# A fused attention, mixer and expert kernel: value products of the last stage begun a step later, output projections queued behind the next projections

## The chip, the cores and the metric

One core of one Trainium2 chip runs the whole program in one launch. The metric is device microseconds of that core; the kernel before took 782.88 us (median of three runs, 781.44 to 784.33). The engines are TensorE (PE, with its weight loads as PEld), VectorE (DVE), ScalarE (ACT), GpSimd (POOL) and SyncE (SP), which issues the DMAs.

## The reference

Three layers on four batches of 576 positions, in float32:

```python
# 1. attention on q, k, v (4, 8, 576, 64): banded part plus a part pooled by 4; 2. mixer over tokens and channels
# 3. four experts, each a causal attention of its own (x is 4 x 576 x 512, wq/wk/wv 512 x 64, wo 64 x 512)
logits = x @ w_gate                                   # the top 2 of 4 get softmax weights w
for e in range(E):
    q = x @ wq[e]; k = x @ wk[e]; v = x @ wv[e]
    scores = np.where(causal, -1e9, scale * (q @ k.transpose(0, 2, 1)))
    a = softmax(scores)                               # max taken off, 1e-9 added to the sum
    ye = a @ v @ wo[e]
    out += mask[..., None] * w[:, :, kk:kk + 1] * ye  # where expert e is one of the top 2
```

## The kernel before, in words

The first two layers fill the first 560 us or so; the change leaves their instructions in the same order on every engine. The last stage is the third layer. It goes through eight pairs, here called pair 0 to pair 7: batch 0 experts 0 and 1, batch 0 experts 2 and 3, batch 1 experts 0 and 1, and so on. Even pairs open a batch, odd pairs close one.

For each pair there are ten score tiles (five tiles of 116, the last of 112, query positions, times two experts), in the order 4, 3, 2, 0, 1 (`TORD`). A loop over 14 steps issues, at step n, the score tile n (`score`: three or more matmuls into PSUM, then on DVE the maximum `nm`, on ACT the exponential into a tile `Pc`, on DVE the normalisation with the gate) and, four steps later (`LAG`), its transposes (`turn`: PE into `pt`, ACT copies into `PT`). When all tiles of one half of the positions are turned, `attend` multiplies `PT` by the values `VV` into `o`: 10 matmul pairs of experts for the later half (at step 9), 6 for the earlier half (at step 13, the pair's last). In the trace these are the `o<-PT,VV` runs of 20 and 12 records.

Beside that, every step takes one item or more from a list `fill`. Its items are the four projections of the next pair (`proj`: K and Q, two halves each, 12 matmuls), for odd pairs also the value projections (`v_proj`) and gates of the next batch, and for even pairs from 2 on the five output projections (`project_out`: 6 matmuls into `wo`, an ACT copy into a tile `y`, a DMA of `y` to the output) of the batch just finished. In pairs 2 and 4 the output projections stand at the head of the list, in pair 6 (`HOLD`) behind the four projections. `split_x` takes each batch's activations apart into `vh` (ACT, `vh<-u`) and `vlo` (POOL); it has six buffers for four tiles per batch, so it is placed where the projections of the batch before have let go of them.

`y` and `Pc` share one tag of eight buffers (`PCB`), PSUM has six single banks and one double one, and SP issues all DMAs in order. A scheduler sets each engine's order from program order, priorities (`ahead`) and its own estimate of durations; each engine then works strictly in that order and waits on semaphores. `chain` keeps the matmuls of one run in their order on PE without a wait.

Of the kernel before, what the change touches and what calls it, by code (L numbers as in the profile page):

```python
# [65 lines left out]
def body(ctx, tc, qT, kT, vw, vp, wt1, wt2, wc1, wc2, wq, wk, wvg, wo, out):  # L66
# [25 lines left out]

        return nc.vector if i < VEC.get(kind, 0) else nc.gpsimd

    def chain(run):

        for x, y in zip(run, run[1:]):
            tc.add_manual_dep(y.ins, x.ins.name, mybir.DependencyInfo(mybir.DependencyClass.NoSync,
                                                                      mybir.DependencyReason.DATA), reason="chain")

    cst = pool("cst")
    ident = cst.tile([128, 128], F32, name="ident")
# [39 lines left out]
    def mm3(ps, terms, first=True, last=True):  # L142
        n = 3 * len(terms)
        i = 0
        for (lh, ll), (rh, rl) in terms:
            for a, c in ((lh, rh), (lh, rl), (ll, rh)):
                nc.tensor.matmul(ps, a, c, start=first and i == 0, stop=last and i == n - 1)  # L147
                i += 1

    def flat(t, shape):  # L150
# [133 lines left out]
    def scores(b, p):  # L284
# [20 lines left out]

        ps = b2("sl")
        for h in range(2):
            nc.tensor.matmul(ps[:, h, :NW * 32].rearrange("p (t k) -> p t k", k=WIN), identb,
                             band[:, None, :].to_broadcast([128, NW // 2, WIN]), start=True, stop=False)
        for w in range(NW):  # L310
            o, g = 64 * (w % 2), 2 * (w // 2)
            cols = slice(KS[w], KS[w] + WIN)

            for h0, h1 in [(0, 2)] if g != NT - 1 else [(0, 1), (1, 2)]:
                bk, c0 = (g + h0) // NT, (g + h0) % NT * WIN
                nc.tensor.matmul(ps[o:o + 64, bk, c0:c0 + (h1 - h0) * WIN].rearrange("p (h k) -> p h k", k=WIN),  # L316
                                 qt[:, cols], kz[:, h0:h1, cols], start=False, stop=(g + h1) % NT == 0)
        sv = ps[:, :, :NW * 32].rearrange("p b (t k) -> p b t k", k=WIN)
        nmx = pa.tile([128, 2, NT], F32, tag="nmx", bufs=3, name="nmx")
# [14 lines left out]
        sd = b2("sd")  # L334
        for h in range(2):
            for c in range(2):
                nc.tensor.matmul(sd[:72, h, c * SD:(c + 1) * SD], qd[64 * h:64 * h + 64, c * 72:(c + 1) * 72],
                                 kd[64 * h:64 * h + 64, :], start=True, stop=True)
        sdv = sd[:72, :, :2 * SD].rearrange("p h (c k) -> p h c k", c=2)
        nd = pa.tile([72, 2, 2], F32, tag="nd", bufs=3, name="nd")  # L340
# [16 lines left out]
    def turns(b, p):  # L357
        P, Pd = SC.pop((b, p))
        PdT = pa.tile([112, 3, SD], F32, tag="PdT", bufs=2, name="PdT")
        pd = b1("pdt")  # L360
        for i, (k0, k) in enumerate(PK):
            k = min(112, 2 * SD - k0)
            for c in range(2):
                o = i * SD + c * 72
                nc.tensor.transpose(pd[:k, o:o + 72], Pd[:, c].rearrange("p h k -> p (h k)")[:, k0:k0 + k], ident[:72, :72])
        nc.scalar.activation(PdT[:, :2].rearrange("p c k -> p (c k)"), pd[:112, :2 * SD], AF.Copy)
        nc.scalar.activation(PdT[:96, 2], pd[:96, 2 * SD:3 * SD], AF.Copy)
        PT = pa.tile([128, NT, 128], F32, tag="PT", bufs=2, name=f"PT{b}_{p}")
        for t0, t1 in ((0, 3), (3, 5)):
            ps = b1("tl")  # L370
            for t in range(t0, t1):
                nc.tensor.transpose(ps[:, (t - t0) * 128:(t - t0 + 1) * 128], P[:, t], ident)
            nc.scalar.activation(PT[:, t0:t1].rearrange("p t q -> p (t q)"), ps[:, :(t1 - t0) * 128], AF.Copy)
        TR[b, p] = (PT, PdT)

    def values(b, p):
        PT, PdT = TR.pop((b, p))
        po = b1("pod")
        vd, vx = Vd[b, p]
        for h in range(2):  # L380
            k = PK[2 * h][1]
            nc.tensor.matmul(po[64 * h:64 * h + 64, :SD], vd[:k, h], PdT[:k, 2 * h], start=True, stop=False)
        nc.tensor.matmul(po[:, :SD], vx.rearrange("p h d -> p (h d)"), PdT[:, 1], start=False, stop=True)
        OdT = pa.tile([128, SD], F32, tag="OdT", bufs=2, name="OdT")
        nc.scalar.activation(OdT, po[:, :SD], AF.Copy)
        up = OdT[:, :, None].to_broadcast([128, SD, 4])
        for w0, w1 in ((0, 4), (4, NW)):
            o = b1("ol")
            s0 = w0 * WQ
            s1 = min(w1 * WQ, S)  # L390
            for w in range(w0, w1):
                q0 = w * WQ
                n = min(WQ, S - q0)
                r0 = 64 * (w % 2) + q0 - KS[w]
                for h in range(2):
                    nc.tensor.matmul(o[64 * h:64 * h + 64, q0 - s0:q0 - s0 + n], Vl[b, p][:, h, w],  # L396
                                     PT[:, w // 2, r0:r0 + n], start=True, stop=True)
            nc.vector.tensor_tensor(U[b][:, p, s0:s1].rearrange("p (g r) -> p g r", r=4),
                                    o[:, :s1 - s0].rearrange("p (g r) -> p g r", r=4),
                                    up[:, s0 // 4:s1 // 4], op=OP.add)  # L400
# [3 lines left out]
    def tok_turn(b, hf):  # L404
        xs = []
        for g in range(3):
            ts = [2 * g, 2 * g + 1] if g < 2 else [4]
            tn = TS[ts[0]]
            ps = b1(f"tx{g}")
            psv = ps.rearrange("p (t d) -> p t d", t=2)  # L410
            for i, t in enumerate(ts):
                for j in range(2):
                    nc.tensor.transpose(psv[:tn, i, j * 128:(j + 1) * 128],
                                        U[b][:, 2 * hf + j, TQ * t:TQ * t + tn], ident)
            hi = pt.tile([TQ, len(ts), 256], F32R, tag=f"xh{g}", bufs=1, name="xh")
            lo = pt.tile([TQ, len(ts), 256], F32R, tag=f"xl{g}", bufs=1, name="xl")
            n = len(ts)
            split(hi[:tn, :n], lo[:tn, :n], psv[:tn, :n])
            xs += [(hi[:tn, i], lo[:tn, i]) for i in range(n)]
        TK[b, hf] = xs  # L420
# [270 lines left out]
    def score(b, p, t, e):  # L691
# [11 lines left out]
            sv = ps[:nq, :, :HS]  # L703
        for ps, a0, a1 in parts:
            m0, m1 = max(d0, a0), min(d0 + nq, a1)
            nc.tensor.matmul(ps[:nq, :a1 - a0], Q[:, qs], K1[:, a0:a1], start=True, stop=False)  # L706
            nc.tensor.matmul(ps[:nq, :a1 - a0], Q[:, qs], K2[:, a0:a1], start=False, stop=m0 >= m1)
            if m0 < m1:
                nc.tensor.matmul(ps[:nq, m0 - a0:m1 - a0], identb[:nq, :nq], caus[:nq, m0 - d0:m1 - d0],  # L709
                                 start=False, stop=True)  # L710
        nm = pc.tile([TQ, 1], F32, tag="nm", bufs=6, name="nm")
        su = pc.tile([TQ, 1], F32, tag="su", bufs=6, name="su")
# [15 lines left out]
    def turn(b, p, t, e):  # L728
# [4 lines left out]
        for c0, c1 in [(0, t + 1)] if t < 4 else [(0, 4), (4, 5)]:  # L733
            pt = b1("pt")
            for c in range(c0, c1):
                nc.tensor.transpose(pt[:TS[c], (c - c0) * TQ:(c - c0) * TQ + nq], P[:nq, c * TQ:c * TQ + TS[c]],  # L736
                                    ident[:nq, :nq])
            v = pt[:, :(c1 - c0) * TQ].rearrange("p (c q) -> p c q", q=TQ)[:, :, :nq]
            m = min(c1, 3)
# [7 lines left out]
    def attend(b, p, s):  # L747
# [4 lines left out]
        q0, q1 = s * HS, (s + 1) * HS  # L752
        o = b1("o")
        cs = [c for c in range(NT) if c * TQ < q1]
        run = []

        for c in cs:
            a = max(q0, c * TQ)
            for e in (1, 0):
                ec = (2 * p + e) * 64  # L760
                run.append(nc.tensor.matmul(o[64 * e:64 * e + 64, a - q0:q1 - q0], ST[b]["VV"][:TS[c], c, ec:ec + 64],  # L761
                                 PT[e][:TS[c], column(c, a):column(c, a) + q1 - a], start=(c == 0), stop=(c == cs[-1])))
        chain(run)
        oh, ol = ST[b]["OT"][p]
        split(oh[:, q0:q1], ol[:, q0:q1], o[:, :HS])

# [17 lines left out]
    if PRE:  # L784
        for k, s in parts:
            proj(0, 1, k, s)
    fill, held, later = [], [], []
    tiles = [(t, e) for t in TORD for e in range(2)]
    for i, (b, p) in enumerate(pairs):
        nxt = pairs[i + 1] if i + 1 < len(pairs) else None  # L790
        if nxt:
# [5 lines left out]
            if nxt[1] == 0:  # L797
                fill += [lambda t=t, n=nxt: v_proj(n[0], t) for t in range(NT)]
                fill += [lambda n=nxt: gates(n[0])]
        if i >= HOLD or nxt is None:  # L800
            fill, held = fill + held, []
        steps = len(tiles) + LAG
        last = nxt is None
        if last:
# [3 lines left out]
                [lambda t=t, b=b: project_out(b, t) for t in range(NT)])  # L808
        wait = [{(t, e) for t, e in tiles if t * TQ < (s + 1) * HS and t * TQ + TS[t] > s * HS} for s in range(2)]
        for n in range(steps):  # L810
            if n < len(tiles):
                with ahead("s"):
                    score(b, p, *tiles[n])
            if n >= LAG:
                with ahead("t"):
                    turn(b, p, *tiles[n - LAG])
                for s in range(2):
                    if tiles[n - LAG] in wait[s]:
                        wait[s].remove(tiles[n - LAG])
                        if not wait[s]:  # L820
                            with ahead("a"):
                                attend(b, p, s)
                            if last:
                                for t in range(NT):
                                    if s in todo[t]:
                                        todo[t].remove(s)
                                        if not todo[t]:
                                            fill.append(lambda t=t: project_out(b, t))
            left = max(1, steps - FRONT - n)
            for _ in range(-(-len(fill) // left)):  # L830
                with ahead("f"):
                    fill.pop(0)()
        fill += later
        later.clear()
    for f in fill:
        f()

# [52 lines left out]
```

## Time and profile before

| | |
|---|---|
| runs before | 782.88 us median (781.44 to 784.33) |
| the profiled execution | 780.84 us, span 779.0 us |
| mean granted TensorE clock | 0.963 of full speed |
| PE busy, whole span | 697.4 us (90%) |
| last stage, from the first value product to the end | 576.9 to 779.0 us |

The profile comes from one execution. A line of the timeline gives start, duration, engine, source line, operation, output and inputs, the number of records merged, and in brackets how long the engine had been idle before it and what it waited for. Busy PE time is modelled at the ends of matmuls, so idle times are the surer reading. A granted clock of 1.00 is 2.4 GHz, 0.50 is 1.2 GHz; a window's figure is a mean over it.

### The profile page before, as it was taken

The page shows a single profiled execution, that of the slowest core. Times are in us where ns is not written, and L with a number is a line of the kernel's source. Part 1 is how long each engine was busy: PE and PEld are TensorE (multiplying, and loading weights), DVE is VectorE, ACT ScalarE, POOL GpSimd, SP SyncE. Part 2 cuts the span into 40 slices and gives each one's busy share as a digit, 9 for nine tenths or more (in the row PEclk, how much of TensorE's full clock was granted, in tenths as well). Part 3 has the DMA queues.
Part 4 walks back from the last instruction along what each step waited for, and adds up shares of the span by engine and source line. Part 5 has one row for each costly group of instructions (what it writes and reads, how often), then busy time and mean ns, then how long its engine had stood idle before and what let it go on. Part 6 is the DMA issues. An engine that isn't in the chain of part 4 may idle for free.

```text
span 779.0 us, 15384 instructions
## 1 busy us (share of the span) xinstructions
PE 697.4 (90%) x5784; PEld 632.3 (81%) x5784; DVE 482.4 (62%) x1203; ACT 398.5 (51%) x1321; POOL 164.8 (21%) x196
## 2 busy tenths in 40 slices
PE   4266889999999999999999999999989989989983
PEld 2245667788899999999999999999979769778762
DVE  3686989555455966854664455443487567577560
ACT  5466686566543625522542233332376466566661
POOL 4477787443101302100200000004030020010000
PEclk9578989999999999999999999999999999999998
DMA  7777755431001301300110010000201111220201
GB/s 215 195 207 206 225 182 167 111 111 47 19 1 33 131 1 59 105 1 1 56 55 1 1 42 14 1 2 1 50 13 32 50 48 28 64 57 4 66 28 61
DMA packets 31586, 52.39 MB, mean 67 GB/s; under 512 B 3544, under 2 KB 16344, under 8 KB 31512
## 3 DMA queue, kind: packets, MB, share of 16 engines
q1 hardware_dynamic: 31512, 51.40, 23.1%
q8 instruction: 46, 0.75, 0.4%
q14 instruction: 28, 0.23, 0.1%
HBM read 41.95 MB, written 4.72 MB: 60 GB/s over the span
## 4 chain that ended last, share of the span: by engine, by line
PE 67%; DVE 11%; DMA 10%; ACT 7%; SPq 2%; issue 2%; ACTq 0%; DVEq 0%
PE c L147 34%; PE proj L147 5%; DMA wc_raw<-in_wc_dram 4%; PE vp L147 4%; PE o L761 4%; PE h L147 4%; DMA out_dram<-y 3%; PE pu L147 3%; PE ol L396 2%; ACT Pc L716 2%; PE sl L316 2%; PE wo L147 2%; PE pt L736 2%; DMA vz<-in_vw_dram 2%; PE s L706 1%
## 5 line engine op out<-in xcount | busy, mean ns | idle before, releaser
L147 PE MATMUL c<-ul,wch 128*128 128x288 f32 x384 | 113.7, 296 | 0.9 <-DVE ul L522 0.9
L147 PE MATMUL c<-uh,wch 128*128 128x288 f32 x384 | 113.5, 296 | 0.4 <-DVE acc L545 0.4
L147 PE MATMUL c<-hh,wch 128*128 128x288 f32 x384 | 113.9, 297 | 0.0
L147 PE MATMUL c<-hl,wch 128*128 128x288 f32 x384 | 113.4, 295 | 0.0
L147 PE MATMUL c<-hh,wcl 128*128 128x288 f32 x384 | 113.2, 295 | 0.0
L147 PE MATMUL c<-uh,wcl 128*128 128x288 f32 x384 | 113.1, 295 | 0.0
L130 ACT ACTIVATE hh<-c 128x288 fp32r<-128x288 f32 x96 | 39.1, 408 | 120.7 <-PE c L147 120.7
L136 DVE SCALAR_TENSOR_TENSOR hl<-c,hh 128x288 fp32r<-128x288 f32 x96 | 43.3, 452 | 63.7 <-ACT hh L130 63.7
L147 PEld LDWEIGHTS c<-ul,wch 128*128 128x128 f32 x384 | 72.4, 188 | 1.8 <-DVE ul L522 1.8
L147 PEld LDWEIGHTS c<-uh,wch 128*128 128x128 f32 x384 | 72.1, 188 | 0.9 <-DVE acc L545 0.9
L147 PEld LDWEIGHTS c<-hl,wch 128*128 128x128 f32 x384 | 72.3, 188 | 0.1
L147 PEld LDWEIGHTS c<-hh,wch 128*128 128x128 f32 x384 | 72.2, 188 | 0.2
L147 PEld LDWEIGHTS c<-hh,wcl 128*128 128x128 f32 x384 | 72.3, 188 | 0.0
L147 PEld LDWEIGHTS c<-uh,wcl 128*128 128x128 f32 x384 | 72.3, 188 | 0.0
L193 POOL TENSOR_TENSOR wc_t<-wc_f,wc_t 128x512 int32<-128x512 int32 x24 | 33.7, 1408 | 168.9 <-ACT wc_t L183 156.6
L521 ACT ACTIVATE uh<-u 128x288 fp32r<-128x288 f32 x128 | 52.9, 441 | 27.4 <-PE c L147 27.4
L522 DVE TENSOR_TENSOR ul<-u,uh 128x288 fp32r<-128x288 f32 x128 | 56.5, 469 | 8.8 <-ACT uh L521 8.7
L327 ACT ACTIVATE P<-sl,nmx 128x64 f32<-128x64 f32 x160 | 48.3, 333 | 19.7 <-DVE nmx L321 19.6
L716 ACT ACTIVATE Pc<-s,nm 112x576 f32<-112x576 f32 (+4 forms) x80 | 44.5, 559 | 25.9 <-DVE nm L713 14.4
L713 DVE TENSOR_REDUCE nm<-s 112x1 f32<-112x576 f32 (+4 forms) x80 | 40.4, 515 | 10.9 <-PE s L709 10.1
L625 POOL TENSOR_TENSOR vlo<-u,vh 128x576 fp32r<-128x576 f32 x16 | 22.6, 1448 | 90.8 <-ACT vh L624 90.8
L761 PE MATMUL o<-PT,VV 116*64 116x288 f32 (+4 forms) x256 | 29.4, 375 | 12.2 <-ACT PT L741 12.2
(171 smaller groups left out, 1828.6 us busy)
## 6 DMA issues: line engine op xcount, KB each, us to landing
wc_raw<-in_wc_dram SPq DMA_DIRECT2D x24, 512.0 KB
vp<-in_vp_dram SPq DMA_DIRECT2D x16, 336.0 KB
vz<-in_vw_dram SPq DMA_DIRECT2D x32, 160.0 KB
qT<-in_qT_dram SPq DMA_DIRECT2D x16, 288.0 KB
kz<-in_kT_dram SPq DMA_DIRECT2D x32, 144.0 KB
kT<-in_kT_dram SPq DMA_DIRECT2D x16, 288.0 KB
K<-K SPq DMA_DIRECT2D x64, 72.0 KB
out_dram<-y SPq DMA_DIRECT2D x16, 232.0 KB
```

The lines of the kernel that those rows point to most:

```text
L130: nc.scalar.activation(hi, src, AF.Relu if relu else AF.Copy, **({"scale": scale} if scale else {}))
L136: nc.vector.scalar_tensor_tensor(lo, src, 0.0, h, op0=OP.max, op1=OP.subtract)
L147: nc.tensor.matmul(ps, a, c, start=first and i == 0, stop=last and i == n - 1)
L193: nc.gpsimd.tensor_tensor(flat(dst, shape).bitcast(I32), f, t.bitcast(I32), op=OP.add)
L316: nc.tensor.matmul(ps[o:o + 64, bk, c0:c0 + (h1 - h0) * WIN].rearrange("p (h k) -> p h k", k=WIN), qt[:, cols], kz[:, h0:h1, cols], start= ...
L327: nc.scalar.activation(P[:, t, h], sv[:, bk, i], AF.Exp, bias=nmx[:, bk, i:i + 1], scale=0.125, accum_out=sm[:, t, h:h + 1])
L521: nc.scalar.activation(hi, u, AF.Copy)
L522: getattr(nc, ULO).tensor_tensor(lo, u, hi.bitcast(F32), op=OP.subtract)
L625: getattr(nc, XLO).tensor_tensor(lo, U[b][:, c], hi.bitcast(F32), op=OP.subtract)
L713: nc.vector.tensor_reduce(nm[:nq], sv, axis=AX.X if t < 4 else AX.XY, op=OP.max, negate=True)
L716: nc.scalar.activation(pv_, sv, AF.Exp, bias=nm[:nq], accum_out=su[:nq])
L761: run.append(nc.tensor.matmul(o[64 * e:64 * e + 64, a - q0:q1 - q0], ST[b]["VV"][:TS[c], c, ec:ec + 64], PT[e][:TS[c], column(c, a):column ...
```

## The change

All matmuls and transposes now go through `mm` and `tp`, which note the last one issued. While `order["on"]` is set (in `attend`), each matmul is kept behind the one issued just before it in the program, the first of the run included. This replaces `chain`, which kept only the run together.

`attend` is no longer called where its last tile is turned, except in the last pair. It goes into `due` and is called at the end of the next step, after that step's score, turn and `fill` items. For the later half that is step 10, in which no score is left. For the earlier half it is step 0 of the next pair.

The output projections of a finished batch are no longer put into `fill` at the end of the odd pair. They wait in `later` and `ready` and join `fill` at step 1 of the even pair, behind its projections.

```diff
+    def behind(ins):
+
+        if order["on"]:
+            tc.add_manual_dep(ins.ins, order["last"].ins.name,
+                              mybir.DependencyInfo(mybir.DependencyClass.NoSync, mybir.DependencyReason.DATA),
+                              reason="order")
+        order["last"] = ins
+
+    def mm(*a, **kw):
+        behind(nc.tensor.matmul(*a, **kw))
...
-        if i >= HOLD or nxt is None:
-            fill, held = fill + held, []
...
         for n in range(steps):
+            now, due = due, []
...
-                        if not wait[s]:
+                        if not wait[s] and not last:
+                            due.append((b, p, s))
+                        elif not wait[s]:
                             with ahead("a"):
                                 attend(b, p, s)
...
+            if n == 1:
+                fill, ready = fill + ready, []
+                if i >= HOLD or last:
+                    fill, held = fill + held, []
             left = max(1, steps - FRONT - n)
             for _ in range(-(-len(fill) // left)):
                 with ahead("f"):
                     fill.pop(0)()
-        fill += later
-        later.clear()
+            for a in now:
+                with ahead("a"):
+                    attend(*a)
+        ready, later = ready + later, []
```

On TensorE at the end of pair 1, the run of the earlier half stood right behind the last two transposes and ahead of the output projections of batch 0 (line 736 is `turn`, 761 `attend`, 147 `mm3`):

```order
L736 MATMUL pt<-ident,Pc 116x116 x2
L761 MATMUL o<-PT_7150,VV 64x288
L761 MATMUL o<-PT_7149,VV 64x288
L761 MATMUL o<-PT_7150,VV 64x172
L761 MATMUL o<-PT_7149,VV 64x172
L761 MATMUL o<-PT_7150,VV 64x56
L761 MATMUL o<-PT_7149,VV 64x56
L147 MATMUL wo<-wo_hi,oh 116x512
L147 MATMUL wo<-wo_lo,oh 116x512
L147 MATMUL wo<-wo_hi,ol 116x512
```

In the changed program twelve matmuls of a K projection stand between those transposes and the run (the last four of them are shown; line 106 is now `mm`, for all):

```order
L106 MATMUL proj<-vh,wk_hi 128x288
L106 MATMUL proj<-vh,wk_hi 128x288
L106 MATMUL proj<-vlo,wk_hi 128x288
L106 MATMUL proj<-vh,wk_lo 128x288
L106 MATMUL o<-PT_7150,VV 64x288
L106 MATMUL o<-PT_7149,VV 64x288
L106 MATMUL o<-PT_7150,VV 64x172
L106 MATMUL o<-PT_7149,VV 64x172
L106 MATMUL o<-PT_7150,VV 64x56
L106 MATMUL o<-PT_7149,VV 64x56
L106 MATMUL proj<-vh,wk_hi 128x288
L106 MATMUL proj<-vlo,wk_hi 128x288
```

The run has moved behind one projection; the output projections have left this place altogether.

On ScalarE at the start of pair 2 there stood the copies of the output projections, one between each two exponentials (line 773 is the copy into `y`, 716 the exponential, 741 and 745 the copies of transposes):

```order
L130 ACTIVATE oh<-o 128x288
L773 ACTIVATE y<-wo 116x512
L716 ACTIVATE Pc,su<-s,nm 112x576
L773 ACTIVATE y<-wo 116x512
L716 ACTIVATE Pc,su<-s,nm 116x464
L773 ACTIVATE y<-wo 116x512
L716 ACTIVATE Pc,su<-s,nm 116x464
L773 ACTIVATE y<-wo 116x512
L741 ACTIVATE PT_7458<-pt 116x3x112
L745 ACTIVATE PT_7458<-pt 116x112
L745 ACTIVATE PT_7458<-pt 112x112
L716 ACTIVATE Pc,su<-s,nm 116x348
```

Now the copies of K and Q stand there (line 140), and four copies `vh` of the next batches (line 634):

```order
L140 ACTIVATE oh<-o 128x288
L140 ACTIVATE K_7831<-proj 64x288
L726 ACTIVATE Pc,su<-s,nm 116x464
L140 ACTIVATE K_7832<-proj 64x288
L140 ACTIVATE Q_7829<-proj 64x288
L634 ACTIVATE vh<-u_91 128x576 x2
L634 ACTIVATE vh<-u_92 128x576
L726 ACTIVATE Pc,su<-s,nm 116x464
L140 ACTIVATE Q_7829<-proj 64x288
L634 ACTIVATE vh<-u_92 128x576
L140 ACTIVATE Q_7830<-proj 64x288
L751 ACTIVATE PT_7449<-pt 116x3x112
```

The `vh` copies came last in pair 2 before, among the copies of Q; they now come first, and the copies into `y` follow from the turn of the first tile on, as they stood and still stand in pair 6. On SP the eight K copies of pairs 2 and 4 now go ahead of the five writes of `y` instead of behind them. Pair 6, the run at its end, and pair 7 keep their order.

## Rows read from the trace of the kernel before

**Rows 1.** The page's first line.
```profile
span 779.0 us, 15384 instructions
```

**Rows 2.** Windows of pairs 1, 2, 4, 6: length; PE, PEld, DVE, ACT, POOL busy; PEclk, DMA.
```profile
581.93:607.42 25.49, 24.49 (x209) 22.62 (x205) 18.85 (x68) 15.60 (x50) 0.11 (x1) 1.00 0.10 24
607.42:638.60 31.18, 26.82 (x179) 21.56 (x175) 17.19 (x50) 18.95 (x56) 5.52 (x4) 0.95 0.21 58
...
664.05:692.52 28.47, 24.40 (x174) 20.26 (x170) 15.41 (x46) 17.68 (x53) 2.80 (x2) 1.00 0.23 64
...
718.63:746.93 28.30, 25.86 (x176) 21.84 (x175) 16.76 (x51) 17.24 (x51) 0.00 (x0) 0.94 0.23 64
```

**Rows 3.** PE's waits, 576.8 to 779: total us, times, longest.
```profile
PE o L761 <- ACT PT L741: 12.2, 14, 2.5
PE s L706 <- DVE Q L138: 3.2, 1, 3.2
PE proj L147 <- ACT Pc L716: 1.9, 2, 0.9
...
PE wo L147 <- ACT y L773: 0.4, 2, 0.2
```

**Rows 4.** PE's timeline, pairs 0 to 6: records behind a wait, and three transposes.
```profile
569.01 0.41 PE L706 MATMUL s<-K,Q 128*116 128x348 f32 x1 [1.12 <-ACT Pc L716]
...
570.36 0.39 PE L706 MATMUL s<-K,Q 128*112 128x288 f32 x1 [0.72 <-DVE Q L138]
...
601.33 0.47 PE L736 MATMUL pt<-ident,Pc 116*116 116x116 f32 x3
602.34 2.25 PE L761 MATMUL o<-PT,VV 116*64 116x288 f32 x20 [0.55 <-ACT PT L741]
...
606.38 1.11 PE L761 MATMUL o<-PT,VV 116*64 116x288 f32 x12 [0.45 <-ACT PT L741]
...
631.57 0.39 PE L706 MATMUL s<-K,Q 128*112 128x288 f32 x1 [3.23 <-DVE Q L138]
...
632.42 3.80 PE L761 MATMUL o<-PT,VV 116*64 116x288 f32 x20
...
687.44 2.26 PE L761 MATMUL o<-PT,VV 116*64 116x288 f32 x20 [2.51 <-ACT PT L741]
...
740.26 3.21 PE L761 MATMUL o<-PT,VV 116*64 116x288 f32 x20 [1.99 <-ACT PT L741]
```

**Rows 5.** ACT's timeline, end of pair 6.
```profile
726.20 0.65 ACT L716 ACTIVATE Pc<-s,nm 116x464 f32<-116x464 f32 x1 [1.33 <-DVE nm L713]
...
731.54 0.60 ACT L773 ACTIVATE y<-wo 116x512 f32<-116x512 f32 x1
...
735.17 0.36 ACT L716 ACTIVATE Pc<-s,nm 116x116 f32<-116x116 f32 x1 [0.88 <-DMA out_dram<-y]
...
738.82 0.46 ACT L716 ACTIVATE Pc<-s,nm 116x232 f32<-116x232 f32 x1 [1.85 <-DMA out_dram<-y]
...
739.75 0.46 ACT L741 ACTIVATE PT<-pt 116x348 f32<-116x348 f32 x1
741.65 0.45 ACT L716 ACTIVATE Pc<-s,nm 116x232 f32<-116x232 f32 x1 [1.45 <-DMA out_dram<-y]
```

**Rows 6.** Chain that ended last, start of pair 3: a projection's twelve matmuls.
```profile
642.50 1.65 PE proj L147 x12
```

**Rows 7.** ACT's timeline in pair 0: two copies `vh`.
```profile
567.09 1.25 ACT L624 ACTIVATE vh<-u 128x576 fp32r<-128x576 f32 x2
```

**Rows 8.** Windows around the first value product of pairs 2, 4, 6, columns as before.
```profile
631.57:636.00 4.43, 4.43 (x25) 2.62 (x25) 2.96 (x8) 2.05 (x7) 2.92 (x3) 0.61 0.01 4
684.00:690.00 6.00, 3.49 (x33) 2.43 (x32) 3.85 (x12) 4.18 (x12) 2.80 (x2) 1.00 0.16 37
740.20:743.50 3.30, 3.24 (x21) 1.85 (x22) 2.09 (x8) 1.27 (x5) 0.00 (x0) 0.68 0.46 138
```

**Rows 9.** DMA busy in 40 slices (tenths of 16 engines), 729.9 to 742.
```profile
DMA  0003222131223212213122221223122222236778
```

More of the change, by code (lines that the diff above doesn't have):

```diff
@@ L93, in spare, with tp @@
         return nc.vector if i < VEC.get(kind, 0) else nc.gpsimd
[L95 to L99, printed above, removed]
+    order = {"on": False, "last": None}
+    def behind(ins):
[6 more added lines that the diff above has]
+        behind(nc.tensor.matmul(*a, **kw))
+    def tp(*a):
+        behind(nc.tensor.transpose(*a))
     cst = pool("cst")
@@ L146, in mm3 @@
             for a, c in ((lh, rh), (lh, rl), (ll, rh)):
-                nc.tensor.matmul(ps, a, c, start=first and i == 0, stop=last and i == n - 1)
+                mm(ps, a, c, start=first and i == 0, stop=last and i == n - 1)
                 i += 1
@@ L307, in scores @@
         for h in range(2):
-            nc.tensor.matmul(ps[:, h, :NW * 32].rearrange("p (t k) -> p t k", k=WIN), identb,
+            mm(ps[:, h, :NW * 32].rearrange("p (t k) -> p t k", k=WIN), identb,
                              band[:, None, :].to_broadcast([128, NW // 2, WIN]), start=True, stop=False)
@@ L315, in scores @@
                 bk, c0 = (g + h0) // NT, (g + h0) % NT * WIN
-                nc.tensor.matmul(ps[o:o + 64, bk, c0:c0 + (h1 - h0) * WIN].rearrange("p (h k) -> p h k", k=WIN),
+                mm(ps[o:o + 64, bk, c0:c0 + (h1 - h0) * WIN].rearrange("p (h k) -> p h k", k=WIN),
                                  qt[:, cols], kz[:, h0:h1, cols], start=False, stop=(g + h1) % NT == 0)
@@ L336, in scores @@
             for c in range(2):
-                nc.tensor.matmul(sd[:72, h, c * SD:(c + 1) * SD], qd[64 * h:64 * h + 64, c * 72:(c + 1) * 72],
+                mm(sd[:72, h, c * SD:(c + 1) * SD], qd[64 * h:64 * h + 64, c * 72:(c + 1) * 72],
                                  kd[64 * h:64 * h + 64, :], start=True, stop=True)
@@ L364, in turns @@
                 o = i * SD + c * 72
-                nc.tensor.transpose(pd[:k, o:o + 72], Pd[:, c].rearrange("p h k -> p (h k)")[:, k0:k0 + k], ident[:72, :72])
+                tp(pd[:k, o:o + 72], Pd[:, c].rearrange("p h k -> p (h k)")[:, k0:k0 + k], ident[:72, :72])
         nc.scalar.activation(PdT[:, :2].rearrange("p c k -> p (c k)"), pd[:112, :2 * SD], AF.Copy)
@@ L371, in turns @@
             for t in range(t0, t1):
-                nc.tensor.transpose(ps[:, (t - t0) * 128:(t - t0 + 1) * 128], P[:, t], ident)
+                tp(ps[:, (t - t0) * 128:(t - t0 + 1) * 128], P[:, t], ident)
             nc.scalar.activation(PT[:, t0:t1].rearrange("p t q -> p (t q)"), ps[:, :(t1 - t0) * 128], AF.Copy)
@@ L381, in values @@
             k = PK[2 * h][1]
-            nc.tensor.matmul(po[64 * h:64 * h + 64, :SD], vd[:k, h], PdT[:k, 2 * h], start=True, stop=False)
-        nc.tensor.matmul(po[:, :SD], vx.rearrange("p h d -> p (h d)"), PdT[:, 1], start=False, stop=True)
+            mm(po[64 * h:64 * h + 64, :SD], vd[:k, h], PdT[:k, 2 * h], start=True, stop=False)
+        mm(po[:, :SD], vx.rearrange("p h d -> p (h d)"), PdT[:, 1], start=False, stop=True)
         OdT = pa.tile([128, SD], F32, tag="OdT", bufs=2, name="OdT")
@@ L395, in values @@
                 for h in range(2):
-                    nc.tensor.matmul(o[64 * h:64 * h + 64, q0 - s0:q0 - s0 + n], Vl[b, p][:, h, w],
+                    mm(o[64 * h:64 * h + 64, q0 - s0:q0 - s0 + n], Vl[b, p][:, h, w],
                                      PT[:, w // 2, r0:r0 + n], start=True, stop=True)
@@ L412, in tok_turn @@
                 for j in range(2):
-                    nc.tensor.transpose(psv[:tn, i, j * 128:(j + 1) * 128],
+                    tp(psv[:tn, i, j * 128:(j + 1) * 128],
                                         U[b][:, 2 * hf + j, TQ * t:TQ * t + tn], ident)
@@ L705, in score @@
             m0, m1 = max(d0, a0), min(d0 + nq, a1)
-            nc.tensor.matmul(ps[:nq, :a1 - a0], Q[:, qs], K1[:, a0:a1], start=True, stop=False)
-            nc.tensor.matmul(ps[:nq, :a1 - a0], Q[:, qs], K2[:, a0:a1], start=False, stop=m0 >= m1)
+            mm(ps[:nq, :a1 - a0], Q[:, qs], K1[:, a0:a1], start=True, stop=False)
+            mm(ps[:nq, :a1 - a0], Q[:, qs], K2[:, a0:a1], start=False, stop=m0 >= m1)
             if m0 < m1:
-                nc.tensor.matmul(ps[:nq, m0 - a0:m1 - a0], identb[:nq, :nq], caus[:nq, m0 - d0:m1 - d0],
+                mm(ps[:nq, m0 - a0:m1 - a0], identb[:nq, :nq], caus[:nq, m0 - d0:m1 - d0],
                                  start=False, stop=True)
@@ L735, in turn @@
             for c in range(c0, c1):
-                nc.tensor.transpose(pt[:TS[c], (c - c0) * TQ:(c - c0) * TQ + nq], P[:nq, c * TQ:c * TQ + TS[c]],
+                tp(pt[:TS[c], (c - c0) * TQ:(c - c0) * TQ + nq], P[:nq, c * TQ:c * TQ + TS[c]],
                                     ident[:nq, :nq])
@@ L754, in attend @@
         cs = [c for c in range(NT) if c * TQ < q1]
-        run = []
+        order["on"] = True
         for c in cs:
@@ L760, in attend @@
                 ec = (2 * p + e) * 64
-                run.append(nc.tensor.matmul(o[64 * e:64 * e + 64, a - q0:q1 - q0], ST[b]["VV"][:TS[c], c, ec:ec + 64],
-                                 PT[e][:TS[c], column(c, a):column(c, a) + q1 - a], start=(c == 0), stop=(c == cs[-1])))
-        chain(run)
+                mm(o[64 * e:64 * e + 64, a - q0:q1 - q0], ST[b]["VV"][:TS[c], c, ec:ec + 64],
+                                 PT[e][:TS[c], column(c, a):column(c, a) + q1 - a], start=(c == 0), stop=(c == cs[-1]))
+        order["on"] = False
         oh, ol = ST[b]["OT"][p]
@@ L786, in body @@
             proj(0, 1, k, s)
-    fill, held, later = [], [], []
+    fill, held, later, ready, due = [], [], [], [], []
     tiles = [(t, e) for t in TORD for e in range(2)]
```

## Prediction

> **What bounds the kernel now.** I read the page first, then cut the last stage into its eight pairs (from the end of one 12-record value run to the end of the next), then asked in each for TensorE's waits and followed those back on ScalarE. The profiled execution took 780.84 us, of which the span is 779.0 [rows 1]; the change touches only the part behind 576.9.
>
> An odd pair is bound by TensorE: pair 1 lasts 25.49 us with 24.49 busy [rows 2], and pairs 3 and 5 read the same. What is idle there is two short waits for ScalarE's copies of the last turned tiles, 0.55 us ahead of the first value run and 0.45 ahead of the second [rows 4]. Even pairs, which carry the output projections, are 3 to 6 us longer: 31.18, 28.47 and 28.30 [rows 2]. In pair 2 TensorE stands for 3.23 us at a score for the next pair, because that score needs the last projected Q, whose copy is late; in pair 4 it stands for 2.51 at the first value run [rows 4]. Both have one wait of about 0.95 at a Q projection and one of 0.2 at an output projection [rows 3]. Pair 6 already works in the order that pairs 2 and 4 get: projections first, output projections behind them. It stands for 1.99 us at the first value run [rows 4].
>
> That last wait matters most here, since it stays. On ScalarE at the end of pair 6 the exponentials wait for the writes of `y`, which share their buffers: 0.88, 1.85 and 1.45 us [rows 5]. ScalarE works in order, so the copy of turned tiles at 739.75, which the first value run needs, stands behind the exponential that waited until 738.82. The `y` it waited for was made at 731.54 to 732.14, so that write took up to 6.7 us to land. Releases come 3.65 and 2.83 us apart.
>
> **The change part by part.**
>
> *Second value run behind a projection.* In pairs 0, 1, 3, 4 and 5 the run waits 0.45 us each (one row of five alike) [rows 4]. Twelve projection matmuls, 1.65 us [rows 6], now go into that time; the copy is done long before they end. Pair 2 has no such wait, since a score already fills it; pair 6 has no projection to put there, and pair 7 is exempt. Gain: 5 x 0.45 = 2.25 us. At worst the wait returns at the next instruction (gain 0): behind the run stand the second half of the K projection and then scores, and ScalarE's `oh` copy now stands behind one or two K copies and ahead of the others. Nothing needs the run's result before the output projections, four steps on at least, so I take the gain whole.
>
> *First value run.* In step 10 no score is left and the list is empty, so only one transpose moves ahead of it. Three transposes take 0.47 us [rows 4], so one covers 0.1 to 0.16 of the wait. Pairs 0, 1, 3 and 5: 4 x 0.1 = 0.4 us. Between 0 and 0.6.
>
> *Pair 2.* The waits of 3.23, 0.95 and 0.2 sum to 4.4 us [rows 3, 4]. They come from the output projections standing first: their copies into `y` stand between the exponentials on ScalarE, the projections and their copies of K and Q slide to the end, and the `vh` copies fall among the last Q copies. With projections first, the last Q is made eight steps earlier, so the 3.23 goes, and with it the buffer wait in the middle. What is late next is pair 6's own wait, 1.99, plus what the early `vh` copies push ScalarE back. There are four, at 1.25 per two [rows 7], 2.5 us; ScalarE has 1.33 idle at that place in pair 6 [rows 5], so 1.2 is left. It runs nearly without a gap from there to the copies into `y`, so I pass the 1.2 on to the writes and to the wait: 3.2. Gain: 4.4 - 3.2 = 1.2 us. From above: the 1.2 is absorbed, gain 2.4. From below: pair 0 is the one place where `vh` copies stand among early copies of Q, and there TensorE waits 1.12 and 0.72 more [rows 4]; with those, 1.99 + 1.2 + 1.84, it is a loss of 0.6.
>
> *Pair 4.* 2.51, 0.95 and 0.2 go, 3.7 us; 1.99 comes. Its two `vh` copies (1.25) fit into the 1.33. Gain 1.7, between 0 (the same wait as now, ScalarE no freer) and 3.1 (only the 0.55 of an odd pair is left).
>
> *The clock.* After the 3.23 of pair 2 the granted clock reads 0.61 over the next 4.4 us, after the 1.99 of pair 6 0.68, after the 2.51 of pair 4 1.00 [rows 8]: half speed for part of the window in two of three. The run behind it takes 3.80 and 3.21 us instead of 2.26 [rows 4], so a drop costs 1.0 to 1.5 us in the run alone. Which of pairs 2 and 4 will be hit can't be read from the length of the wait. One drop between them, as now, costs nothing; none gains 1.5, two lose 1.5.
>
> *Queues.* The K copies on SP go ahead of the writes of `y`, whose data come later anyway; the last two `y` of pairs 2 and 4 block exponentials of the next pair, which come more than 8 us later, longer than the 6.7 above. Same instructions otherwise, and nothing ahead of 560 us moves.
>
> Sum: 2.25 + 0.4 + 1.2 + 1.7 = 5.5 us off. Against the profiled execution that is 780.84 - 5.5 = 775.3. That execution lies 2.0 under the median of the runs, so the forecast in the runs' measure is 782.88 - 5.5 = 777.4 us. As a second way to the same number, pair 6 without its 0.45 and its drop (1.4 with the slowed transposes behind it) would be 26.4; pair 4 by its terms becomes 28.47 - 1.7 - 0.45 = 26.3.
>
> **The rivals.** A measurement of this kernel can tell about 0.5%, 3.9 us, from no change, so faster is under 779.0 and slower over 786.8.
>
> *The writes keep up (773).* If the writes of `y` landed within the step time of about 2.1 us (the copies into `y` are as far apart in pair 6), no exponential would wait and pairs 2 and 4 would keep only an odd pair's 0.55: 4.4 - 0.55 and 3.7 - 0.55, together 7.0 instead of 2.9, with the 2.65 of the value runs 9.65, so 773.2, or 771.7 if the clock stays up as well. Against it: while the four 116-row writes are under way the DMA engines read 2 tenths of 16 busy, about 3, and only the last, 112-row write lifts that to 7 or 8 [rows 9]; releases are 2.8 to 3.7 us apart. The Trainium skill, "DMA: Bandwidth & Descriptors", section "Why a DMA increments its semaphore by 16 and not by 1", says that a DMA uses the largest number of engines up to 16 that divides its row count, which is 4 for 116 rows and 16 for 112, and the trace agrees. By its figure of about 27 GiB/s per engine I estimate 2.0 us for a 232 KB write, by which this rival would hold; the releases here are slower than that.
>
> *The waits only move (780.2).* The value runs give their 2.65, and pairs 2 and 4 stay as long as they are: the early `vh` and K copies crowd ScalarE as in pair 0, and the `y` wait grows by as much as the others shrink. For it: that pair 6 is no shorter than pair 4 today (28.30 against 28.47), with the order that pair 4 gets. Against it: pair 6 has a clock drop and pair 4 none.
>
> *Slower: the writes of `y` block ScalarE (788.5).* Today they come early in pairs 2 and 4, and eight steps follow to make up for them; afterwards they come last, right ahead of the value run. If all three waits for them (0.88 + 1.85 + 1.45 = 4.2) fall on TensorE, and the `vh` copies in full (2.5 and 1.25), the wait in pair 2 is 6.7 and in pair 4 5.5 where 4.4 and 3.7 went: 4.1 lost; a second clock drop adds 1.5, and if the second runs gain nothing, since ScalarE is behind, the sum is 788.5. It decides once those two waits pass 8.1 + 2.65 = 10.7 us together. Pair 6 speaks against it: three such waits on ScalarE, 1.99 on TensorE.
>
> *The change doesn't do what it says*: for the first run of each pair this is so, and it is in the sum.
>
> **How the numbers follow.** The forecast has 0.55 (775 to 779.5 by its own bounds, nine tenths of it under 779.0), the writes that keep up 0.15, waits that only move 0.23, slower 0.07. So faster 0.65, same 0.28, slower 0.07. The range 773.0 to 781.5 holds the forecast's bounds, most of the first rival and the second.
>
> **What would show it.** In the profile after: the 0.45 ahead of the second value run gone in pairs 0, 1, 3, 4, 5, with K projections there; no wait for Q at a score; a wait of 2 to 3.2 us ahead of the first value run in pairs 2, 4 and 6, released by the copy of turned tiles, and on ScalarE exponentials waiting for `y` just before it; pair 4 at 26.3 us or, with a drop, 27.8; odd pairs at about 25. I am wrong if pairs 2 and 4 are as long as before, if the wait at the first run is under 1 us, or if TensorE stands at the start of pair 2 behind the `vh` copies.

## The result, and the profile after

The changed kernel takes 771.13 us (median of 5 runs, 770.64 to 771.66) where the kernel before takes 782.88: a ratio of 0.985, 95% interval 0.983 to 0.987. It is faster by 11.75 us. The forecast was 777.4 us, the range 773.0 to 781.5: the direction was right, the gain is twice what was forecast, and the time lies below the range.

The profiled execution of the changed kernel took 771.66 us with a span of 769.9, against 780.84 and 779.0 before. Its first 571 us, which the change does not touch, are 2.07 us longer than the same work before (the score that waits 1.12 us stands at 571.08 instead of 569.01 [rows 4]); from there to the end it is 11.2 us shorter. The following text is about these 11.2.

Windows of the changed kernel, columns as in [rows 2]; each goes from the start of one 12-record value run to the start of the next: pairs 1, 2, 4, 6 and 7, and what lies behind the last value run.

```profile
584.68:609.53 24.85, 24.40 (x205) 22.62 (x204) 18.91 (x68) 16.27 (x52) 0.11 (x1) 1.00 0.10 25
609.53:635.79 26.26, 24.41 (x175) 20.81 (x174) 16.91 (x50) 19.09 (x56) 5.78 (x4) 1.00 0.23 69
...
660.67:686.78 26.11, 24.68 (x176) 20.85 (x175) 17.24 (x50) 17.86 (x53) 2.81 (x2) 1.00 0.25 69
...
711.65:736.76 25.11, 22.95 (x163) 19.25 (x163) 16.16 (x50) 16.13 (x50) 0.00 (x0) 1.00 0.25 71
736.76:753.32 16.56, 13.16 (x99) 9.88 (x99) 10.05 (x38) 10.70 (x38) 0.00 (x0) 1.00 0.01 2
753.32:769.90 16.58, 5.46 (x30) 3.89 (x30) 0.46 (x1) 1.99 (x4) 0.00 (x0) 0.80 0.23 71
```

The same cut of the kernel before, pairs 2, 4, 5 and 6:

```profile
606.38:637.56 31.18, 26.82 (x175) 21.55 (x175) 17.24 (x52) 18.71 (x55) 5.52 (x4) 0.95 0.21 58
...
663.01:691.48 28.47, 24.41 (x169) 20.26 (x169) 16.07 (x49) 16.84 (x51) 2.80 (x2) 1.00 0.23 64
691.48:717.60 26.12, 25.11 (x211) 23.27 (x211) 19.50 (x71) 16.92 (x54) 0.00 (x0) 1.00 0.10 24
717.60:745.90 28.30, 25.86 (x175) 21.84 (x176) 17.42 (x53) 17.24 (x51) 0.00 (x0) 0.94 0.23 64
```

Pair 2 went from 31.18 to 26.26 us, pair 4 from 28.47 to 26.11, an odd pair from about 25.45 to 24.85. Pair 6's window now starts behind a projection of 12 matmuls, so 1.65 us are to be added to its 25.11: 26.76, from 28.30. Pair 4's window before held 169 matmuls where pairs 2 and 6 have 175, and pair 5's held some six more than an odd pair's 205, so that it was 0.66 us longer than pair 3 (25.45): pair 4 gained about 3.0, not 2.4. With 4.92 (pair 2), 3.0, 1.55 (pair 6) and three times 0.6 that is 11.3; pair 0, pair 7 (16.59 before) and the tail (16.52 before) kept their lengths.

Busy and idle tell two kinds of gain apart. In pair 2 the idle time of TensorE fell from 31.18 - 26.82 = 4.36 to 26.26 - 24.41 = 1.85 us, and its busy time for the same 175 matmuls from 26.82 to 24.41. Most of the second difference, 2.41 us, is the clock: before, the 4.43 us behind the wait had a granted clock of 0.61 on average [rows 8], which is worth (1 - 0.61) x 4.43 = 1.7 us, and now pair 2 has no such stretch. The other 0.7 us is busy time at full clock. Pair 4, whose clock was 1.00 both times, lost 0.4 us of that kind (24.41 and 0.66 for the six matmuls before, 24.68 now). In pair 6 the idle time is about as it was (2.44 and 2.16), while busy fell by 25.86 - 22.95 - 1.65 = 1.26 at a clock of 0.94 before and 1.00 now. In pair 4 most of what went is idle time: 4.06 before, 1.43 now.

TensorE's longest waits of the changed kernel from 571 to 770 (columns as in [rows 3]), and its records behind them:

```profile
PE o L106 <- ACT PT L751: 8.2, 9, 1.5
PE pt L109 <- DVE su L727: 1.6, 2, 1.2
...
PE wo L106 <- ACT Pc L726: 0.6, 1, 0.6
```

```profile
604.52 2.25 PE L106 MATMUL o<-PT,VV 116*64 116x288 f32 x20 [0.45 <-ACT PT L751]
...
609.53 1.10 PE L106 MATMUL o<-PT,VV 116*64 116x288 f32 x12
...
618.11 0.49 PE L106 MATMUL wo<-wo_hi,oh 128*116 128x512 f32 x1 [0.56 <-ACT Pc L726]
...
630.78 2.25 PE L106 MATMUL o<-PT,VV 116*64 116x288 f32 x20 [1.29 <-ACT PT L751]
...
681.36 2.25 PE L106 MATMUL o<-PT,VV 116*64 116x288 f32 x20 [1.29 <-ACT PT L751]
...
732.36 2.25 PE L106 MATMUL o<-PT,VV 116*64 116x288 f32 x20 [1.50 <-ACT PT L751]
```

The value runs' waits fell from 14 to 9 and from 12.2 us to 8.2. The second run (609.53) waits for nothing; the wait for Q at a score of pair 2 is gone; what is left in even pairs stands at the first value run, 1.29, 1.29 and 1.50, and every run of 20 takes 2.25 us, also in pairs 2 and 6, where it took 3.80 and 3.21 [rows 4]. What releases it, on ScalarE in pair 2:

```profile
622.76 0.63 ACT L783 ACTIVATE y<-wo 116x512 f32<-116x512 f32 x1
...
627.00 0.60 ACT L783 ACTIVATE y<-wo 116x512 f32<-116x512 f32 x1 [0.69 <-DMA out_dram<-y]
...
629.34 0.45 ACT L726 ACTIVATE Pc<-s,nm 116x232 f32<-116x232 f32 x1 [1.40 <-DMA out_dram<-y]
629.69 0.19 ACT L726 ACTIVATION_READ_ACCUMULATOR Pc<-s,nm 116x1 f32 x1
629.79 0.59 ACT L783 ACTIVATE y<-wo 112x512 f32<-112x512 f32 x1
630.26 0.62 ACT L751 ACTIVATE PT<-pt 116x348 f32<-116x348 f32 x2
```

It is the pattern of [rows 5]: the `y` made at 622.76 leaves its buffer only by 629.34, ScalarE stands 1.40 us for it, and the copy of turned tiles that the value run needs comes behind. The chains of both kernels (in order of time: start, us, what) hold such a write in each even pair. Before:

```profile
615.42 7.63 DMA out_dram<-y
...
672.05 7.59 DMA out_dram<-y
...
732.17 6.27 DMA out_dram<-y
```

After:

```profile
623.42 5.82 DMA out_dram<-y
...
676.02 6.76 DMA out_dram<-y
...
726.81 7.03 DMA out_dram<-y
```

The first two rows of before are what the prediction did not look at: it laid the losses of pairs 2 and 4 to the order of the work, and the chain shows writes there too. ScalarE's exponentials waited for writes of `y` in pair 2 of before as well:

```profile
ACT Pc L716 <- DMA out_dram<-y: 3.3, 3, 1.4
```

After the change:

```profile
ACT Pc L726 <- DMA out_dram<-y: 2.2, 2, 1.4
...
ACT y L783 <- DMA out_dram<-y: 0.7, 1, 0.7
```

(waits of ScalarE from 600 to 640; total us, times, longest). So ScalarE stands for the writes about as long after the change as before: 2.9 us against 3.3 in pair 2, and 10.1 against 10.7 over the whole last stage. What fell is the part of this that reaches TensorE. Before, the chain leads from the write at 615.42 over the copies of K and Q to the score at 631.57, which waits 3.23 us; after, from the write at 623.42 to the value run at 630.78, which waits 1.29.

### The profile page after: what moved, and what is told of

Same layout as the page of the kernel before. It is cut to its first block, busy times and chain, and to the rows that moved or that the text cites. A ratio compares the mean times of both kernels' runs of the same rounds, so it can differ in the third digit from the quotient of the medians.

```text
span 769.9 us, 15382 instructions
## 1 busy us (share of the span) xinstructions
PE 698.3 (91%) x5784; PEld 634.7 (82%) x5784; DVE 482.4 (63%) x1203; ACT 397.7 (52%) x1321; POOL 166.6 (22%) x196
## 4 chain that ended last, share of the span: by engine, by line
PE 71%; DVE 11%; DMA 9%; ACT 4%; issue 2%; SPq 1%; ACTq 0%; DVEq 0%
PE c L106 35%; PE proj L106 7%; PE vp L106 4%; PE h L106 4%; PE s L106 3%; DMA wc_raw<-in_wc_dram 3%; PE o L106 3%; PE pu L106 3%; DMA out_dram<-y 3%; PE sl L106 2%; DMA vz<-in_vw_dram 2%; PE ol L106 2%; PE pt L109 2%; PE wo L106 2%; DVE wc_f L198 1%
## 5 line engine op out<-in xcount | busy, mean ns | idle before, releaser
L106 PE MATMUL s<-K,Q 128*112 128x288 f32 (+3 forms) x192 | 43.1, 325 | 3.0 <-DVE Q L148 1.6
L729 DVE TENSOR_SCALAR Pc<-Pc,su,gw 112x576 f32<-112x576 f32 (+4 forms) x80 | 38.4, 481 | 2.4
```

Of the source, the lines that this page charges most:

```text
L106: behind(nc.tensor.matmul(*a, **kw))
L729: nc.vector.tensor_scalar(P[:nq, :n], P[:nq, :n], su[:nq], ST[b]["W"][:nq, t, 2 * p + e:2 * p + e + 1], op0=OP.mult, op1=OP.mult)
```

## The experiments

Two theories were put against each other. **W** (the prediction's, widened): in even pairs TensorE waits for ScalarE, whose exponentials wait in order for slow writes of `y`; what the change does is to put other work between a write and the exponential that needs its buffer, and a shorter wait also keeps the clock up (by the rows above, ScalarE's waits for the writes hardly shrank). **S**, the rival: the order of the steps alone decides, the value runs' later start or the projections' place, and writes only happen to be there. The kernel before took 783.33 us (17 runs) beside the first four kernels and 783.5 (11 runs) beside the others. A second measure is the last stage in the one profiled execution of each kernel, from pair 0's first score of 348 columns to the end: 212.4 us before (212.5 in a second execution) and 201.2 after (201.1), 11.2 less.

**Output projections alone.** The kernel before, with only this part of the change:

```
-    fill, held, later = [], [], []
+    fill, held, later, ready = [], [], [], []
...
-        if i >= HOLD or nxt is None:
-            fill, held = fill + held, []
...
+            if n == 1:
+                fill, ready = fill + ready, []
+                if i >= HOLD or last:
+                    fill, held = fill + held, []
...
-        fill += later
-        later.clear()
+        ready, later = ready + later, []
```

> Only the output projections of batches 0 and 1 go behind the next projections; both value runs stay where they were. Theory A (most of the 11.8 us comes from this move, through shorter waits in pairs 2 and 4): 774 to 777 us, the wait for the last Q in pair 2 gone, a wait of 1.3 to 2 us ahead of the first value run in pairs 2, 4 and 6, the 0.45 ahead of every second run still there. Rival B (most of it comes from beginning the value runs a step later): 779 to 782 us.

Measured: 773.5 us (773.08 to 776.36), ratio 0.988, interval 0.986 to 0.991. That is 9.8 us of the whole change's 12.2 by the same runs of before, slightly below the 774 to 777 of Theory A; by the trace's last stage, 204.9 us, it is 7.5 of 11.2. Value runs of pair 2, TensorE:

```profile
630.75 2.25 PE L761 MATMUL o<-PT,VV 116*64 116x288 f32 x20 [1.41 <-ACT PT L741]
...
634.79 1.10 PE L761 MATMUL o<-PT,VV 116*64 116x288 f32 x12 [0.45 <-ACT PT L741]
```

The first waits are those of the changed kernel (1.41, 1.38, 1.52), the wait for Q is gone and no run of 20 is slowed; the 0.45 of the second runs is all still there.

**Value runs alone.** The changed kernel with its output projections put ahead of all but one projection again:

```
-                fill, ready = fill + ready, []
+                fill, ready = ready + fill, []
```

> Only the value runs begin a step later; the output projections of batches 0 and 1 stand ahead of all but the first of the next projections, as near to their old place as they can come behind the run they need. Theory A: 779 to 781 us, the 0.45 ahead of second runs gone, pairs 2 and 4 about as long as before. Rival B: 772 to 776 us.

Measured: 779.28 us (774.5 to 781.73), ratio 0.994, interval 0.992 to 0.996. TensorE, pairs 2, 4 and 6:

```profile
630.75 0.78 PE L106 MATMUL s<-K,Q 128*112 128x288 f32 x4 [3.08 <-DVE Q L148]
631.52 3.90 PE L106 MATMUL o<-PT,VV 116*64 116x288 f32 x20
...
686.62 3.90 PE L106 MATMUL o<-PT,VV 116*64 116x288 f32 x20 [2.38 <-ACT PT L751]
...
739.78 2.96 PE L106 MATMUL o<-PT,VV 116*64 116x288 f32 x20 [1.89 <-ACT PT L751]
```

The wait for Q is back, and the run of 20 is slowed in all three pairs. By the runs the later second run is worth about 4 us (interval 2.8 to 6.2; they scatter over 7 us). The trace doesn't bear that out: its last stage takes 212.4 us, as before. The odd pairs are shorter (pair 3 takes 24.82 us instead of 25.45), but pair 4, whose run of 20 is now slowed, takes 30.29 instead of 28.47. The two parts add up to 13.9 us by the runs and 7.5 by the traces, where the change is worth 12.2 and 11.2. So both measures give the output projections the larger part, and what the later runs add alone stays open.

**The writes made quick.** The changed kernel, with each 116-row write of `y` cut into 112 and 4 rows:

```
-        nc.sync.dma_start(out[b, ts], y[:TS[t], :DM])
+        nc.sync.dma_start(out[b, t * TQ:t * TQ + 112], y[:112, :DM])
+        if TS[t] > 112:
+            nc.sync.dma_start(out[b, t * TQ + 112:t * TQ + TS[t]], y[112:TS[t], :DM])
```

> The changed kernel, with each write of 116 rows issued as one of 112 rows and one of 4. Theory W (what is left of the wait ahead of the first value run in pairs 2, 4, 6 is set by how slowly the writes of y land): the waits of 1.29, 1.29 and 1.50 us fall to 0.45, the exponentials no longer wait for writes, and the last writes end sooner: 765 to 769 us. Rival C (it is set by ScalarE's own load of copies): waits stay at 1.2 to 1.5, only the tail gains: 768 to 771 us.

Measured: 761.51 us (759.91 to 761.83), ratio 0.972 to the kernel before, interval 0.969 to 0.975: 9.6 us under the changed kernel, the fastest of all, and less than either theory held. DMA busy from 618 to 632 in 40 slices, in tenths of 16 engines, and GB/s, first in the changed kernel, then with the split:

```profile
DMA  0000000000000222312222222222222222222359
GB/s 0 0 0 0 0 0 0 0 0 0 0 0 6 70 35 59 41 41 64 70 82 94 94 105 99 94 94 105 99 105 99 99 105 99 105 94 94 117 170 281
```

```profile
DMA  0000000000059600993001981002981007940000
GB/s 0 0 0 0 0 0 0 0 0 0 0 164 269 234 12 0 257 293 129 0 0 47 275 287 70 0 0 76 263 287 53 0 0 205 263 182 6 0 0 0
```

Writes that trickled on some 3 of 16 engines, several at a time and together at about 100 GB/s, become bursts on nearly all engines at 260 to 290, and each is over before the next. By the rule on rows that the prediction quoted (the Trainium skill, "DMA: Bandwidth & Descriptors", section "Why a DMA increments its semaphore by 16 and not by 1"), a write of 112 rows uses 16 engines and one of 116 uses 4; these two rows agree. No exponential waits for a write any more, and the first runs of pairs 1 to 6 wait only what is left in an odd pair:

```profile
629.32 2.25 PE L106 MATMUL o<-PT,VV 116*64 116x288 f32 x20 [0.45 <-ACT PT L751]
```

Of the 9.6 us, 5.6 come from the tail: from the last value run to the end it is 10.96 us instead of 16.58, since the last writes are quick too. So 4 are what the slow writes still cost in pairs 2, 4 and 6.

**The writes out of the exponentials' way.** Twelve buffers instead of eight for the exponentials and `y`, once in the changed kernel, once in the kernel before, whose order on TensorE and ScalarE stays as it was:

```
-PCB = 8
+PCB = 12
```

> The changed kernel, with twelve buffers for P and y where eight were; the writes themselves stay as they are. Theory W: the waits ahead of the first value run in pairs 2, 4, 6 fall to 0.45 and no exponential waits for a write, the tail stays: 766 to 769 us. Rival C: waits of 1.2 to 1.5 stay, 770 to 772 us.

> The kernel before with twelve buffers for P and y; ScalarE and TensorE keep the order of before word for word. Theory W (the long waits of pairs 2 and 4 were exponentials of ScalarE waiting for writes of y, 3.3 and 3.2 us, handed on to TensorE): the wait for the last Q in pair 2 and the one ahead of the first value run in pair 4 fall under 1 us, no clock drop there, 769 to 774 us. Rival O (they come from the order itself, K and Q copies late and the vh copies among them): the waits stay over 2 us, 779 to 782 us.

Measured: 766.88 us (765.64 to 768.11; ratio 0.979, interval 0.977 to 0.982) and 772.71 (771.29 to 775.6; 0.988, interval 0.985 to 0.991). The writes are as slow as ever and the tail keeps its 16.65 us, but no exponential waits for them. In the changed kernel the first runs of pairs 1 to 6 wait 0.45. In the kernel before, pairs 2 and 4:

```profile
627.21 0.39 PE L706 MATMUL s<-K,Q 128*112 128x288 f32 x1 [1.98 <-DVE Q L138]
627.99 3.88 PE L761 MATMUL o<-PT,VV 116*64 116x288 f32 x20
...
680.74 2.25 PE L761 MATMUL o<-PT,VV 116*64 116x288 f32 x20 [1.42 <-ACT PT L741]
```

W met its range of times here, but not its waits: it had them fall under 1 us with no clock drop, and they are 1.98 and 1.42, with the run of pair 2 still slowed. So of before's 3.23 at the score, 1.25 was the writes' and 1.98 is the order's: with output projections first, the last Q is late even when no write is in the way. The four kernels side by side, in us (runs, and in brackets the last stage by trace):

| | eight buffers | twelve buffers |
|---|---|---|
| order of before | 783.5 (212.4) | 772.71 (204.6) |
| new order | 771.13 (201.2) | 766.88 (197.2) |

The change is worth 11.8 us with eight buffers and 5.8 with twelve by the runs, 11.2 and 7.4 by the traces. A third to a half of what it gains is thus a remedy for the slow writes, and the rest, the order, is there without them: each theory is right for a part. The slow writes cost the order of before 10.8 us by the runs and the new order 4.3, although ScalarE waits for them about as long in both. So it is not, as W had it, that exponentials find their buffers sooner; their waits now stand where less of them reaches TensorE.

**The writes made slower.** The changed kernel, with each 116-row write cut into 106 and 10 rows:

```
-        nc.sync.dma_start(out[b, ts], y[:TS[t], :DM])
+        m = 106 if TS[t] == TQ else TS[t]
+        nc.sync.dma_start(out[b, t * TQ:t * TQ + m], y[:m, :DM])
+        if TS[t] > m:
+            nc.sync.dma_start(out[b, t * TQ + m:t * TQ + TS[t]], y[m:TS[t], :DM])
```

> The changed kernel with each write of 116 rows issued as one of 106 rows and one of 10, so that most of it runs on fewer DMA engines. Theory W: the writes take about twice as long, the waits ahead of the first value run in pairs 2, 4 and 6 grow to 4 to 8 us each with clock drops behind them, the tail grows: 785 to 805 us, slower than before. Rival C (ScalarE's own load sets those waits): 771 to 776 us.

Measured: 795.06 us (794.24 to 796.54), ratio 1.016, interval 1.013 to 1.019. From 618 to 634 DMA busy reads 1 tenth of 16 engines for most of the time that the writes are under way. By the rule on rows of the Trainium skill quoted above, a write of 106 rows uses 2 engines, with which this agrees. ScalarE's waits from 571 on, and the value run of pair 2:

```profile
ACT Pc L726 <- DMA out_dram<-y: 24.6, 8, 3.6
```

```profile
633.09 4.28 PE L106 MATMUL o<-PT,VV 116*64 116x288 f32 x20 [4.75 <-ACT PT L751]
```

Slower writes do reach TensorE in this order: its first runs wait 4.75, 3.96 and 3.96, the clock falls behind each, and the tail takes 23.3 us. It is the prediction's slower rival, and its mechanism is real; it only needs writes slower than those of this kernel.

**The clock, once more.** Both kernels were run a second time, without a change of the code.

> The kernel before again, for the place of the clock drops. If a drop follows from the length of the wait ahead of it: again behind the 3.2 us of pair 2 and the 2.0 of pair 6, and possibly behind the 2.5 of pair 4. If it falls by chance: other pairs.

> The changed kernel again, for the same: no drop behind waits of 1.3 to 1.5 us in pairs 2, 4 and 6 if the length decides, one or two if it is chance.

Measured: 782.48 and 769.04 us. Before, the clock fell behind the waits of pairs 2 and 6 (3.22 and 1.81) and not behind that of pair 4 (2.53), as in the first trace. After, it fell in none of the three (waits 1.33, 1.30, 1.77), as in the first. The first value runs, before and then after:

```profile
634.82 3.25 PE L761 MATMUL o<-PT,VV 116*64 116x288 f32 x20
...
689.34 2.25 PE L761 MATMUL o<-PT,VV 116*64 116x288 f32 x20 [2.53 <-ACT PT L741]
...
741.95 3.60 PE L761 MATMUL o<-PT,VV 116*64 116x288 f32 x20 [1.81 <-ACT PT L741]
```

```profile
628.06 2.26 PE L106 MATMUL o<-PT,VV 116*64 116x288 f32 x20 [1.33 <-ACT PT L751]
...
678.66 2.25 PE L106 MATMUL o<-PT,VV 116*64 116x288 f32 x20 [1.30 <-ACT PT L751]
...
729.86 2.26 PE L106 MATMUL o<-PT,VV 116*64 116x288 f32 x20 [1.77 <-ACT PT L751]
```

In two executions of each kernel the drops thus came with the kernel, and their loss is counted as part of the change. Whether a third execution would agree was not tried. In pair 6 the waits without a drop (1.77) and with one (1.81) are so close that the length alone does not explain it.

## Why the prediction fell short, step by step

*Second value runs, 2.25: right in kind and about right in size.* The 0.45 is gone in pairs 0, 1, 3, 4 and 5. In the odd pairs it is a gain, with the 0.1 of the first run: 25.45 to 24.85. In pair 0 nothing comes of it: its first run waited 0.99 before, and now the turns ahead of it wait 1.22 for VectorE's `su`.

*Clock, "one drop between them, as now, costs nothing": the step that failed most.* The prediction gave pairs 2 and 4 one drop between them and held pair 6 unchanged. There was none in any of the three, in two traces. A drop had cost 1.7 us in pair 2 and 1.3 in pair 6, 3.0 together; the prediction had priced one at 1.0 to 1.5 and counted none as gained. In the last stage 11.2 - 5.5 = 5.7 us are missing from the forecast, and the clock is about half of it. Another 1.1 us is busy time at full clock (0.7 in pair 2, 0.4 in pair 4), for which the prediction had no term; what makes it is not shown.

*Pair 2, "what is late next is 3.2": the second failing step.* The wait for Q and the buffer wait went as forecast. What came is 1.29 at the first run and 0.56 at an output projection, 1.85 in all: the `vh` copies cost TensorE 0.56 at that place and are not passed on to the writes and the wait. 1.35 us of the gap.

*Pair 4, 1.99 left: mis-sized.* 1.29 stands there. By idle time, without the second run's 0.45, 4.06 - 0.45 - 1.43 = 2.2 us went where 1.7 were forecast: 0.5 us of the gap.

*Pair 6, "unchanged".* Its wait was 1.99 and 1.81 in the two traces before, 1.50 and 1.77 after, though the order ahead of it in the pair is the same; by idle time that is 0.3 us. With only the output projections moved it was 1.52 and no drop followed; with only the value runs moved it was 1.89, and a drop followed. So it goes with the output projections of the earlier pairs; by what path was not settled. With it, and with the 0.55 that pair 0 did not give, the gap is 3.0 + 1.1 + 1.35 + 0.5 + 0.3 - 0.55 = 5.7 us. The other 0.6 us of the 6.3 between forecast and median is how the profiled executions stand to their medians and the 2.07 of the first 571 us.

*The second way to the sum.* It set pair 4's 28.47 beside pair 6's 28.30, and pair 5 as equal to pair 1. But pair 4's window lacked six matmuls, and pair 5, with 26.12 us, had them: for the same work pair 4 was about 0.66 longer. That the two ways met at 26.3 and 26.4, and that 26.11 was measured, is luck.

*What bounds the kernel: half read.* The prediction saw in pair 6 that slow writes hold up ScalarE and that this would be what remains. It is, as the quick writes showed by taking away what was left. It did not see that pairs 2 and 4 suffered from the same writes, 3.3 us on ScalarE in pair 2, and that in the new order much less of such waits would reach TensorE. The twelve buffers show both: they alone took 10.8 us off the kernel before, and 4.3 off the changed one.

*The rivals.* "The writes keep up" gave 771.7 with the clock up, which is nearly the time, and for the wrong reason: writes still take 5.8 to 7.0 us in the chain, and when they do keep up the time is 761.5. "The waits only move" is refuted on TensorE by the idle time of pairs 2 and 4, down 2.5 and 2.6 us; on ScalarE the waits for writes did only move. The slower rival needs writes like those of the 106-row kernel.

## What to carry to other kernels

When an engine that works in order shares a buffer pool with data that wait to be written out, follow its waits to the DMA before touching the order: the chain of waits names the write, and the width of the write (the DMA row, in tenths of 16 engines) tells whether it is the thing to mend. An equal wait on that engine can cost the bottleneck much or little, by what stands behind it in the order. Here cutting one row count so that it uses all engines, added to the change, gave nearly as much (9.6 us) as the reordering (11.8), and it also shortened the tail, which no reordering and no buffer had touched. And when a wait may become shorter, price the lower clock behind it as well, over the whole stretch that runs at it and not over one run of matmuls.

## What the runs showed of the hardware

The clock's answer to a wait is not in its length alone. The 2.51 and 2.53 us waits in pair 4 of before had none of their matmuls slowed, twice, while 1.81 and 1.98 us waits elsewhere had, and 2.38 us in the same pair 4 when only the value runs were moved; behind waits of 1.77 and less in pairs 2, 4 and 6 the run of 20 took 2.25 us in every trace. What sets pair 4 of before apart stays open.

With the 106-row writes the profile reads a granted clock of 0.95 in stretches where every other trace reads 1.00, already between 500 and 560 us, which the edit doesn't touch; there TensorE's busy time is the same 58.87 us, but undisturbed value runs take 2.33 instead of 2.25. Some of that kernel's 24 us may be this; its three waits and its tail are not.
